# Reordering one step of a fused retention and shrink kernel: another order of the engines' work in the steps with 256-column up products, GpSimd's sums one step behind

## The chip, the cores and the metric

One core of a Trainium2 chip runs the whole program in one launch. The metric is device time in microseconds (us), the median of a few executions. Beside it stands one profiled execution, whose span (first to last instruction) is a little shorter than its own time.

## The reference, cut to what matters

Two parts in a row. The first is a retention block: for 4 batches, 8 heads, 768 positions and head size 64 it keeps a decaying state and reads it with q. Its output, seen as 3072 tokens of 512 values, is the input x of the second part:

```python
h = x @ w_in            # 512 -> 2048
g = h - np.tanh(h)
out = g @ w_out         # 2048 -> 512
```

This case is about the second part, and of that about the stretch in which the first part is already over.

## The kernel before, in words

**Tiling.** The tokens are cut into 12 groups n of 256, the 2048 columns of `h` into 8 pairs m2 of 2 x 128. A tile (n, m2) is 128 partitions x 512 values of `h`: it is made by "up" products on TensorE into PSUM, turned into `g` by ScalarE and VectorE, and consumed by "down" products on TensorE. All is float32. The queues of the engines are in the order in which the program is written out (the schedule is manual): each engine works through its own list, and waits are semaphores between the lists.

**Seven products for eight.** Up and down products use Strassen's scheme (in Winograd's form): 7 block products in place of 8, paid for by sums of blocks. For up products the sums of token blocks are made on GpSimd (`up_tokens`, `block_tokens`, lines 776 to 824), the sums of weights earlier. For down products GpSimd makes four sums of each `g` tile (`fast_sums`, lines 637 to 646, four instructions); products 1, 2 and 4 take `g` itself, products 3, 5, 6 and 7 take a sum.

**Down products as a stream.** `waiting` is the list of tiles whose down products are still to be issued, n by n; the eight tiles of one n are a run and accumulate into one set of PSUM pieces. `next_products(k)` (line 877) issues the next k of the stream. When a tile's last product is issued, `feed()` (line 907) issues GpSimd's sums for those of the next three tiles that are in the set `shrunk`. When a run ends, `fast_end(n)` (line 723) reads the accumulators: `p1` (a copy on ScalarE), then on VectorE `c11`, `v`, and then, as pieces taken from the list `ending`, `w`, `c22`, `x`, `c21`, `c12`, with the stores. Groups 7 to 10 use the same accumulators, so the next run's first products wait for these reads.

**Steps with 128-column products** (n = 4 to 7, lines 1086 to 1158; for n = 6 and 7 the down products come from the stream). A step makes one tile: 8 up products ("U": 1, 5, 7, 6, two matmuls each), `up_take` (ScalarE copies the PSUM bank), `up_pairs` (GpSimd), some down products, 6 more up matmuls ("V": 2, 3, 4) into the same bank, which therefore wait for the copy; `up_add` on VectorE, tanh and square on ScalarE, and the rest of the shrink. At (n, m2) = (7, 2) the four token sums of the first block are issued, in a row.

**Steps with 256-column products** (lines 1180 to 1222; called block steps j = 0 to 15 here). A block is two groups n: block 4 is groups 8 and 9 (j = 0 to 7), block 5 is groups 10 and 11 (j = 8 to 15). Step j makes two tiles at once, A of group 2b and B of group 2b+1, with m2 = j mod 8: U is 8 matmuls of 256 columns, `block_take` copies both banks (ScalarE, two copies), `block_pairs` adds them (GpSimd), V is 6 matmuls into the copied banks, `block_add` adds to them (VectorE: first one for A, then two for B). Then, for each tile: tanh `th` and square `u`, further squares `q0` and `q1` and the mask `large` on ScalarE, and five operations on VectorE, called f0 to f4 here: f0 `th = h - th` (line 502), f1 and f2 multiply by factors (lines 506, 515), f3 multiplies by `u` into `g` (line 543), f4 `copy_predicated` puts `th` where |h| is large (line 544). The last steps of tile B (q1, large, f2 to f4) are done in the next step, after U (`rest(*before)`). Down products are issued in two places of a step: 4 after U, and after V as many as a running count `aim` asks for (10 a step in block 4, 14 in block 5). For the next block, one of four token sums is issued in each of the steps j = 4 to 7.

Of the kernel before, what the change touches and what calls it, by code (L numbers as in the profile page):

```python
# [10 lines left out]
I32 = mybir.dt.int32  # L11
U32 = mybir.dt.uint32
U16 = mybir.dt.uint16
AF = mybir.ActivationFunctionType
# [17 lines left out]
def kernel(  # L32
# [437 lines left out]
    def shrink_begin(n, m2):  # L470
        hp = hps[n, m2]
        u, th = (work(x, 2) for x in ("u", "th"))
        if n < FAST_UP:
            nc.scalar.activation(u, hp, AF.Square)
            nc.scalar.activation(th, hp, AF.Tanh)  # L475
        else:
            nc.scalar.activation(th, hp, AF.Tanh)  # L477
            nc.scalar.activation(u, hp, AF.Square)
        shrinking[n, m2] = [u, th]

    def shrink_factor(n, m2):
        q0 = work("q0", 1)
        nc.scalar.activation(q0, shrinking[n, m2][0], AF.Square, bias=bias0)  # L483
        shrinking[n, m2].append(q0)

    def shrink_factors(n, m2):
        u = shrinking[n, m2][0]
        if n < FAST_UP:
            shrink_factor(n, m2)
        large, q1 = work("large", 2), work("q1", 1)  # L490
        nc.scalar.activation(q1, u, AF.Square, bias=bias1, scale=math.sqrt(A))  # L491
        nc.scalar.activation(large, u, AF.Relu, bias=bias_m)  # L492
        shrinking[n, m2] += [q1, large]

    def shrink_multiply(n, m2):
        shrink_two(n, m2)
# [1 line left out]

    def shrink_two(n, m2):
        hp = hps[n, m2]  # L500
        th = shrinking[n, m2][1]
        nc.vector.tensor_tensor(th, hp, th, op=ALU.subtract)  # L502

    def shrink_third(n, m2):
        hp = hps[n, m2]
        nc.vector.scalar_tensor_tensor(hp, in0=shrinking[n, m2][2], scalar=C0, in1=hp,  # L506
                                       op0=ALU.add, op1=ALU.mult)

    def shrink_last_factor(n, m2):

        hp = hps.pop((n, m2))
        q1 = shrinking[n, m2][3]
        g = gT[n, m2] = new_g(n, m2)
        dst = hp if n < FAST_UP else g.rearrange("p i t -> p (i t)")
        nc.vector.scalar_tensor_tensor(dst, in0=q1, scalar=A * C1, in1=hp, op0=ALU.add,
                                       op1=ALU.mult)
        shrinking[n, m2].append(dst)

    units = []

# [17 lines left out]
        return units.pop(0) if units else next(rooms_for_g)  # L538

    def shrink_end(n, m2):  # L540
        u, th, _, _, large, src = shrinking.pop((n, m2))
        flat = gT[n, m2].rearrange("p i t -> p (i t)")
        nc.vector.tensor_tensor(flat, src, u, op=ALU.mult)
        nc.vector.copy_predicated(flat, large.bitcast(I32), th)  # L544
# [267 lines left out]
    def block_tokens(b):  # L812


        x = xT[b]
        b11, b12, b21, b22 = (x[:, ds(2 * c, 2), ts(i, TH)] for c in range(2) for i in range(2))
        room = op.tile([P, 2, 2, TH], F32, tag="sum", name=f"x_block_{b}")
        t2, t3 = (room[:, i] for i in range(2))
        t4 = odd_room[3].rearrange("p (b c t) -> p b c t", b=2, c=2)[:, b % 2]
        x_of["block", b] = (b11, b21, b22, t4, b12, t2, t3)  # L820
        return [
            lambda d=d, x=x, y=y: nc.gpsimd.tensor_tensor(d, x, y, op=ALU.subtract)
            for d, x, y in ((t3, b22, b12), (b12, b12, b11), (t2, b22, b12), (t4, b21, t2))
        ]
# [219 lines left out]
    for n in range(FAST_UP + 1, PAIRED):  # L1044
        at_ = FIRST_UP - 1 if n == FAST_UP + 1 else PAIRS * (n - 1) + 2
        with_sums.setdefault(at_, []).append(lambda n=n: more_tokens(n))
    def first_block():
        for make in block_tokens(PAIRED // 2):
            make()

    with_sums.setdefault(PAIRS * (PAIRED - 1) + 2, []).append(first_block)
    before = None

    def middle():
# [31 lines left out]
    for s in range(BEGUN, steps.index((PAIRED, 0, True, False))):  # L1086
        n, m2, first, last = steps[s]
        fast = n >= FAST_UP
        ci = with_chunk.get(s)

        falls_back = s == FALL or s in behind_up
        lag = LAG + int(s >= FALL)
        if ci is not None and not falls_back:
            chunk_step(ci)
        if s + 1 in with_chunk:
            for which in range(2):
                scale(with_chunk[s + 1] + 3, which, nc.gpsimd)
        for i in with_weights.get(s, []):
            convert(i)
        if fast:  # L1100
            fast_up(n, m2, (1, 5, 7, 6))
            up_take(n, m2)
        else:
            for i in range(2):
                up(n, m2, i)
        if falls_back and ci is not None:
            chunk_step(ci)
        if before and ci is not None:
            turn_and_see(ci)
        if ci == NCH - 2:  # L1110
            outputs(ci + 1)
            see(ci + 1)
        for i in with_weights.get(s, []):
            load_weights(i + 3)
        waiting.append(steps[s])
        if fast:
            if before and ci is None:
                shrink_factors(*before)
                shrink_last_factor(*before)
            up_pairs()  # L1120
            for make in with_sums.get(s, []):
                make()
            if n < PAIRED - 2:
                downs(lag, 0)
            else:
                next_products(4)
                end_run()
            fast_up(n, m2, (2, 3, 4))
            up_add(n, m2)
            shrink_begin(n, m2)  # L1130
            if before:
                shrink_end(*before)
                if before[0] >= FAST:
                    shrunk.add(before)
                    if n < PAIRED - 2:
                        fast_sums(*before)
                    else:
                        feed()
            if n < PAIRED - 2:
                downs(lag, 1)  # L1140
            else:
                next_products(2)
                end_run()
            end_some(1 + 2 * (n == PAIRED - 1))
            shrink_two(n, m2)
            before = n, m2
            if s + 1 not in with_chunk:
                middle()
        else:
            shrink_begin(n, m2)  # L1150
            shrink_factors(n, m2)
            shrink_multiply(n, m2)
            downs(lag)
            shrink_last_factor(n, m2)
            shrink_end(n, m2)
            for make in with_sums.get(s, []):
                make()
# [2 lines left out]


    def begin(n, m2):
        shrinking[n, m2] = [work(x, 2) for x in ("u", "th")]

    def activated(n, m2, i):
        nc.scalar.activation(shrinking[n, m2][i], hps[n, m2], (AF.Square, AF.Tanh)[i])

    def rest(n, m2):
        shrink_factors(n, m2)
        shrink_last_factor(n, m2)  # L1170
        shrink_end(n, m2)
        shrunk.add((n, m2))
        feed()

    for n in range(PAIRED, 2 * NB):
# [4 lines left out]
    for j in range((NB - FIRST_BLOCK) * PAIRS):  # L1180
        b, m2 = FIRST_BLOCK + j // PAIRS, j % PAIRS
        one, other = (2 * b, m2), (2 * b + 1, m2)
        for i, x in enumerate((one, other)):
            hps[x] = bank("h", "h_%d_%d" % x) if j % 2 else fast_o[i]
        block_up(b, m2, (1, 7, 5, 6))
        block_take(b, m2)
        block_pairs()
        near = left_in_run() <= 7
        next_products(left_in_run() if near else 4)
        rest(*before)  # L1190
        end_run()
        end_some(len(ending))
        if m2 == PAIRS // 2 and b + 1 < NB:
            tokens = block_tokens(b + 1)
        block_up(b, m2, (2, 4, 3))
        aim += 10 if j < PAIRS else 14
        if not near:
            next_products(min(left_in_run(), aim - made[0]))
        if m2 >= PAIRS // 2 and tokens:
            tokens.pop(0)()  # L1200
        block_add(b, m2, [(0, 1)])
        begin(*one)
        activated(*one, 1)
        activated(*one, 0)
        block_add(b, m2, [(1, 0), (1, 1)])
        begin(*other)
        activated(*other, 1)
        shrink_two(*one)
        end_run()
        end_some(len(ending))  # L1210
        shrink_factor(*one)
        shrink_third(*one)
        shrink_factors(*one)
        shrink_last_factor(*one)
        shrink_end(*one)
        shrunk.add(one)
        feed()
        activated(*other, 0)
        shrink_two(*other)
        shrink_factor(*other)  # L1220
        shrink_third(*other)
        before = other
    rest(*before)
    next_products(left_in_run())
    end_run()
    end_some(len(ending))
    LAST = 3
# [63 lines left out]
```

## Time and profile before

| | before |
|---|---|
| median of 3 runs (lowest, highest) | 696.23 us (694.76, 696.40) |
| profiled execution: its own time, its span | 696.99 us, 694.9 us |
| TensorE busy, share of the span | 684.3 us, 98% |
| VectorE busy | 534.2 us, 77% |
| ScalarE busy | 427.3 us, 61% |
| GpSimd busy | 358.3 us, 52% |
| TensorE clock granted | full in every slice |

The steps (6, 0) to (7, 7) lie at about 387 to 480 us of the span, the block steps at 480 to 661 us, and then come the last down products, whose last matmul ends at about 691.7 us. In the profile PE is TensorE, PEld its weight loads, DVE VectorE, ACT ScalarE, POOL GpSimd, SP the queue of the stores and loads. "Idle before <-releaser" is the time for which an engine stood still and what it waited for.

### The profile page before, as it was taken

Reading aid. Unit: us, or ns where it says so; the run is one execution under the profiler, and the core shown is the slowest. Engines: PE = TensorE matmul, PEld = TensorE weight load, DVE = VectorE, ACT = ScalarE, POOL = GpSimd, SP = SyncE. Lnnn points to the kernel's source line nnn. Section 1 sums busy time; section 2 is a strip of 40 time slices with the busy share of each in tenths; the row PEclk is TensorE's granted clock in tenths of the full one; section 3 lists DMA queues with packets and bytes.
Section 4 is the critical chain, followed back from the end, with each engine's and each line's share of the span. In section 5 each row is a group of like instructions: output and inputs, shape, how many; then the busy total and the mean of one; then the engine's idle time right before and its main releaser. Section 6 shows DMA issues by size and latency. Waiting matters only on the chain.

```text
span 694.9 us, 15471 instructions
## 1 busy us (share of the span) xinstructions
PE 684.3 (98%) x6092; PEld 556.4 (80%) x6092; DVE 534.2 (77%) x879; ACT 427.3 (61%) x817; POOL 358.3 (52%) x492
## 2 busy tenths in 40 slices
PE   8999999999999999999999999999999999999998
PEld 5776666667667667789999999989888888888887
DVE  4899989988988965577776687787879888758741
ACT  3687677776766755456555566656766556557510
POOL 1632455444455586887853464554454456444371
PEclk9999999999999999999999999999999999999999
DMA  8992368958878557500000000000000000000000
GB/s 225 232 276 57 92 153 224 228 145 231 236 173 236 149 159 199 138 33 1 1 1 16 17 1 16 16 0 32 1 1 31 1 1 30 1 0 31 1 31 31
DMA packets 119544, 59.89 MB, mean 86 GB/s; under 512 B 101680, under 2 KB 112560, under 8 KB 119472
## 3 DMA queue, kind: packets, MB, share of 16 engines
q1 hardware_dynamic: 116736, 50.08, 27.9%
q10 hardware_dynamic: 2736, 8.83, 3.4%
q8 instruction: 48, 0.79, 0.5%
q14 instruction: 24, 0.20, 0.1%
HBM read 35.83 MB, written 14.68 MB: 73 GB/s over the span
## 4 chain that ended last, share of the span: by engine, by line
PE 88%; DMA 3%; POOL 3%; SPq 2%; ACT 2%; DVE 2%; issue 1%; ACTq 0%; DVEq 0%; POOLq 0%
PE h L464 15%; PE o L552 15%; PE h L793 12%; PE fast_t L692 11%; PE y L692 8%; PE fast_o L832 7%; PE h L832 6%; PE fast_o L692 5%; PE y L398 3%; PE last_h L692 1%; PE s L349 1%; PE s L343 1%; SPq L159 1%; DMA rows<-apart 1%; DMA raw<-in_moe_w_in_dram 1%
## 5 line engine op out<-in xcount | busy, mean ns | idle before, releaser
L464 PE MATMUL h<-xT,w 128*128 128x256 f32 x512 | 117.9, 382 | 0.7 <-ACT xT L444 0.7
L552 PE MATMUL o<-w,g 128*128 128x512 f32 x256 | 116.5, 596 | 0.0
L464 PEld LDWEIGHTS h<-xT,w 128*128 128x128 f32 x512 | 95.9, 190 | 22.4 <-issue 9.1
L552 PEld LDWEIGHTS o<-w,g 128*128 128x128 f32 x256 | 47.5, 190 | 46.2 <-issue 43.0
L483 ACT ACTIVATE q<-u,tab 128x512 f32<-128x512 f32 x88 | 63.7, 724 | 4.5 <-DVE fast_o L506 2.1
L502 DVE TENSOR_TENSOR th<-h,th 128x512 f32<-128x512 f32 x72 | 49.2, 683 | 20.2 <-ACT th L475 17.7
L477 ACT ACTIVATE th<-h 128x512 f32<-128x512 f32 x32 | 19.1, 597 | 73.1 <-DVE h L810 73.1
L208 POOL TENSOR_TENSOR low<-low,power 128x512 f32<-128x512 f32 x26 | 34.1, 1313 | 57.8 <-DVE power L201 42.1
L491 ACT ACTIVATE q<-u,tab 128x512 f32<-128x512 f32 x88 | 63.6, 722 | 0.0
L492 ACT ACTIVATE large<-u,tab 128x512 f32<-128x512 f32 x88 | 62.8, 714 | 0.0
L544 DVE COPY_PREDICATED g<-large,th 128x512 f32<-128x512 int32 x62 | 54.6, 880 | 6.2
L506 DVE SCALAR_TENSOR_TENSOR h<-q,h 128x512 f32<-128x512 f32 x72 | 49.7, 690 | 6.1 <-ACT q L483 6.1
L842 POOL TENSOR_TENSOR fast_head<-fast_head 128x512 f32<-128x512 f32 x16 | 21.4, 1339 | 63.9 <-ACT fast_head L838 63.9
L642 POOL TENSOR_TENSOR s<-g 128x128 f32<-128x128 f32 x38 | 17.8, 469 | 57.5 <-DVE g L544 56.7
L217 POOL TENSOR_TENSOR w<-low,head 128x512 f32<-128x512 f32 x28 | 36.6, 1307 | 14.7 <-DVE low L208 7.6
L793 PEld LDWEIGHTS h<-xT,w 128*128 128x128 f32 x256 | 38.0, 191 | 6.2 <-ACT fast_head L798 1.9
L793 PE MATMUL h<-xT,w 128*128 128x128 f32 x256 | 39.6, 277 | 0.7 <-ACT fast_head L798 0.7
L808 DVE TENSOR_TENSOR h<-h,fast_head 128x256 f32<-128x256 f32 x32 | 13.8, 432 | 33.6 <-PE h L793 25.5
L803 POOL TENSOR_TENSOR fast_head<-fast_head 128x256 f32<-128x256 f32 x32 | 23.4, 730 | 27.5 <-ACT fast_head L798 27.5
L282 POOL TENSOR_TENSOR q<-q,tab 128x512 f32<-128x512 f32 x16 | 17.1, 1066 | 38.7 <-DMA q<-in_q_dram 32.8
L282 POOL TENSOR_TENSOR v<-v,tab 128x512 f32<-128x512 f32 x21 | 24.3, 1157 | 21.3 <-DMA v<-in_v_dram 20.2
L444 ACT COPY xT<-y 128x256 f32<-128x256 f32 x48 | 15.5, 378 | 29.9 <-PE y L398 29.9
(297 smaller groups left out, 1793.2 us busy)
## 6 DMA issues: line engine op xcount, KB each, us to landing
rows<-apart ACTq DMA_DIRECT2D x16, 512.0 KB, 4.5
k<-in_k_dram SPq DMA_DIRECT2D x24, 256.0 KB, 4.4
q<-in_q_dram SPq DMA_DIRECT2D x24, 256.0 KB, 4.7
v<-in_v_dram SPq DMA_DIRECT2D x24, 256.0 KB, 5.7
raw<-in_moe_w_out_dram SPq DMA_DIRECT2D x12, 512.0 KB, 4.3
out_dram<-sum SPq DMA_DIRECT2D x22, 256.0 KB, 2.2
raw<-in_moe_w_in_dram SPq DMA_DIRECT2D x14, 256.0 KB, 4.2
raw<-in_moe_w_in_dram SPq DMA_DIRECT2D x28, 128.0 KB, 4.1
```

What stands on the lines that cost most here:

```text
L282: engine.tensor_tensor(out_, t, g, op=ALU.mult)
L464: nc.tensor.matmul(hp, w1[:, c, ts(2 * m2 + i, P)], xT[n // 2][:, c, ts(n % 2, TH)], start=(begins and c == 0), stop=(c == NC - 1), skip_g ...
L483: nc.scalar.activation(q0, shrinking[n, m2][0], AF.Square, bias=bias0)
L491: nc.scalar.activation(q1, u, AF.Square, bias=bias1, scale=math.sqrt(A))
L492: nc.scalar.activation(large, u, AF.Relu, bias=bias_m)
L502: nc.vector.tensor_tensor(th, hp, th, op=ALU.subtract)
L506: nc.vector.scalar_tensor_tensor(hp, in0=shrinking[n, m2][2], scalar=C0, in1=hp, op0=ALU.add, op1=ALU.mult)
L544: nc.vector.copy_predicated(flat, large.bitcast(I32), th)
L552: nc.tensor.matmul(o_p[n, j], gT[n, m2][:, i, ts(j, P)], w2[:, 2 * m2 + i], start=(first and i == 0), stop=(last and i == 1))
L692: nc.tensor.matmul(accs[n][k], left[k - 1], right, start=first and k in (1, 6, 7, 4), stop=last, skip_group_check=True)
L793: nc.tensor.matmul(hps[n, m2][:, ts(PLACE[k], P)], s_of[m2][k - 1][:, c], x_of[n][k - 1][:, c], start=(k == 1 and c == 0), stop=(c == 1), ...
L832: nc.tensor.matmul(hps[2 * b + i, m2][:, ts(place, TH)], s_of[m2][k - 1][:, c], x_of["block", b][k - 1][:, c], start=(k in (1, 5) and c == 0),
```

## The change

It rewrites the loop over block steps. The order within a step is now a string of pieces, worked through for each step; `-` is tile B of the step before, `A` and `B` the two tiles of this one.

```diff
-        block_up(b, m2, (1, 7, 5, 6))
-        block_take(b, m2)
-        block_pairs()
-        near = left_in_run() <= 7
-        next_products(left_in_run() if near else 4)
-        rest(*before)
-        end_run()
-        end_some(len(ending))
...
-        block_up(b, m2, (2, 4, 3))
-        aim += 10 if j < PAIRS else 14
-        if not near:
-            next_products(min(left_in_run(), aim - made[0]))
...
-        shrink_end(*one)
-        shrunk.add(one)
-        feed()
-        activated(*other, 0)
-        shrink_two(*other)
-        shrink_factor(*other)
-        shrink_third(*other)
+        aim += AIM[j]
+        for piece in order.split():
+            block_pieces[piece](b, m2, one, other, before)
         before = other
```

```python
order = """U M c P q1- s l- f2- V f3- aA thA uA q0A E aB f0A x f4- q1A f1A thB f2A S uB f0B lA f3A f4A q0B f1B"""
AIM = (9, 14, 8, 10, 15, 11, 11, 8, 15, 13, 14, 15, 13, 12, 16, 8)

def more_products():                       # piece E
    if not ended:
        some = min(left_in_run(), aim - made[0])
        next_products(left_in_run() if left_in_run() - some < 6 else some)

def end_sums():                            # piece S
    end_run()
    end_some(len(ending))

def ripe():                                # piece s
    shrunk.update(fresh)
    fresh.clear()
    feed()
```

U and V are the up products, M is `next_products(4)`, c `block_take`, P `block_pairs`, x a token sum of the next block, aA and aB `block_add`; l is `large`. A tile enters `fresh` when its f4 is issued, and `shrunk` only at the next s, so GpSimd's sums for it are issued a step later.

In the steps with 128-column products two things change. The token sums of the first block are spread, one each over (7, 2) to (7, 5). And the down products are grouped otherwise where few are left in a run:

```diff
-                next_products(4)
+                near = left_in_run() if left_in_run() <= 6 else 4
+                next_products(near)
                 end_run()
...
-                next_products(2)
-                end_run()
+                if near == 4:
+                    next_products(6 - 4)
+                    end_run()
```

The last lines after the loop do the remaining pieces of the last tile B, then the rest of run 10, as before. The dictionary in place of a list in `shrinking` changes no instruction.

More of the change, by code (lines that the diff above doesn't have):

```diff
@@ L478, in shrink_begin @@
             nc.scalar.activation(u, hp, AF.Square)
-        shrinking[n, m2] = [u, th]
+        shrinking[n, m2] = {"u": u, "th": th}
     def shrink_factor(n, m2):
         q0 = work("q0", 1)
-        nc.scalar.activation(q0, shrinking[n, m2][0], AF.Square, bias=bias0)
-        shrinking[n, m2].append(q0)
+        nc.scalar.activation(q0, shrinking[n, m2]["u"], AF.Square, bias=bias0)
+        shrinking[n, m2]["q0"] = q0
     def shrink_factors(n, m2):
-        u = shrinking[n, m2][0]
+        u = shrinking[n, m2]["u"]
         if n < FAST_UP:
@@ L492, in shrink_factors @@
         nc.scalar.activation(large, u, AF.Relu, bias=bias_m)
-        shrinking[n, m2] += [q1, large]
+        shrinking[n, m2].update(q1=q1, large=large)
     def shrink_multiply(n, m2):
@@ L500, in shrink_two @@
         hp = hps[n, m2]
-        th = shrinking[n, m2][1]
+        th = shrinking[n, m2]["th"]
         nc.vector.tensor_tensor(th, hp, th, op=ALU.subtract)
@@ L505, in shrink_third @@
         hp = hps[n, m2]
-        nc.vector.scalar_tensor_tensor(hp, in0=shrinking[n, m2][2], scalar=C0, in1=hp,
+        nc.vector.scalar_tensor_tensor(hp, in0=shrinking[n, m2]["q0"], scalar=C0, in1=hp,
                                        op0=ALU.add, op1=ALU.mult)
@@ L511, in shrink_last_factor @@
         hp = hps.pop((n, m2))
-        q1 = shrinking[n, m2][3]
+        q1 = shrinking[n, m2]["q1"]
         g = gT[n, m2] = new_g(n, m2)
@@ L516, in shrink_last_factor @@
                                        op1=ALU.mult)
-        shrinking[n, m2].append(dst)
+        shrinking[n, m2]["src"] = dst
     units = []
@@ L540, in shrink_end @@
     def shrink_end(n, m2):
-        u, th, _, _, large, src = shrinking.pop((n, m2))
+        u, th, large, src = (shrinking[n, m2][x] for x in ("u", "th", "large", "src"))
+        del shrinking[n, m2]
         flat = gT[n, m2].rearrange("p i t -> p (i t)")
@@ L1046, with first_block @@
         with_sums.setdefault(at_, []).append(lambda n=n: more_tokens(n))
[L1047 to L1051, printed above, removed]
+    begun_tokens = []
+    def first_block(i):
+        if not i:
+            begun_tokens.extend(block_tokens(PAIRED // 2))
+        begun_tokens.pop(0)()
+    for i in range(4):
+        with_sums.setdefault(PAIRS * (PAIRED - 1) + 2 + i, []).append(lambda i=i: first_block(i))
     before = None
@@ L1162, in begin, with activated @@
     def begin(n, m2):
[L1163 to L1172, printed above, removed]
+        shrinking[n, m2] = {x: work(x, 2) for x in ("u", "th")}
+    def activated(n, m2, x, how):
+        nc.scalar.activation(shrinking[n, m2][x], hps[n, m2], how)
@@ new lines, in tanh, with shrink_q1, shrink_large, shrink_gated @@
+    def tanh(n, m2):
+        begin(n, m2)
+        activated(n, m2, "th", AF.Tanh)
+    def shrink_q1(n, m2):
+        q1 = work("q1", 1)
+        nc.scalar.activation(q1, shrinking[n, m2]["u"], AF.Square, bias=bias1, scale=math.sqrt(A))
+        shrinking[n, m2]["q1"] = q1
+    def shrink_large(n, m2):
+        large = work("large", 2)
+        nc.scalar.activation(large, shrinking[n, m2]["u"], AF.Relu, bias=bias_m)
+        shrinking[n, m2]["large"] = large
+    def shrink_gated(n, m2):
+        u, src = (shrinking[n, m2][x] for x in ("u", "src"))
+        nc.vector.tensor_tensor(gT[n, m2].rearrange("p i t -> p (i t)"), src, u, op=ALU.mult)
@@ new lines, in shrink_small @@
+    def shrink_small(n, m2):
+        u, th, large, src = (shrinking[n, m2][x] for x in ("u", "th", "large", "src"))
+        del shrinking[n, m2]
+        nc.vector.copy_predicated(gT[n, m2].rearrange("p i t -> p (i t)"),
+                                  large.bitcast(I32), th)
+        fresh.append((n, m2))
+    def more_products():
[3 more added lines that the diff above has]
+    def end_sums():
+        end_run()
+        end_some(len(ending))
@@ new lines, in some_tokens @@
+    def some_tokens(b, m2):
+        if m2 == PAIRS // 2 and b + 1 < NB:
+            tokens.extend(block_tokens(b + 1))
+        if tokens:
+            tokens.pop(0)()
+    of_tile = {
+        "th": tanh, "u": lambda *x: activated(*x, "u", AF.Square), "q0": shrink_factor, "q1": shrink_q1,
+        "l": shrink_large, "f0": shrink_two, "f1": shrink_third, "f2": shrink_last_factor,
+        "f3": shrink_gated, "f4": shrink_small,
+    }
+    block_pieces = {
+        "U": lambda b, m2, *_: block_up(b, m2, (1, 7, 5, 6)),
+        "V": lambda b, m2, *_: block_up(b, m2, (2, 4, 3)),
+        "c": lambda b, m2, *_: block_take(b, m2),
+        "P": lambda *_: block_pairs(),
+        "s": lambda *_: ripe(),
+        "x": lambda b, m2, *_: some_tokens(b, m2),
+        "M": lambda *_: next_products(4),
+        "E": lambda *_: more_products(),
+        "S": lambda *_: end_sums(),
+        "aA": lambda b, m2, *_: block_add(b, m2, [(0, 1)]),
+        "aB": lambda b, m2, *_: block_add(b, m2, [(1, 0), (1, 1)]),
+        **{x + "A": lambda b, m2, one, *_, f=f: f(*one) for x, f in of_tile.items()},
+        **{x + "B": lambda b, m2, one, other, *_, f=f: f(*other) for x, f in of_tile.items()},
+        **{x + "-": lambda *at_, f=f: f(*at_[-1]) for x, f in of_tile.items()},
+    }
@@ L1173, in rest @@
+    order = """U M c P q1- s l- f2- V f3- aA thA uA q0A E aB f0A x f4- q1A f1A thB f2A S uB f0B lA f3A f4A q0B f1B"""
+    AIM = (9, 14, 8, 10, 15, 11, 11, 8, 15, 13, 14, 15, 13, 12, 16, 8)
+    fresh = []
+    def ripe():
+        shrunk.update(fresh)
+        fresh.clear()
         feed()
@@ L1184 @@
             hps[x] = bank("h", "h_%d_%d" % x) if j % 2 else fast_o[i]
-        block_up(b, m2, (1, 7, 5, 6))
-        block_take(b, m2)
-        block_pairs()
-        near = left_in_run() <= 7
-        next_products(left_in_run() if near else 4)
-        rest(*before)
-        end_run()
-        end_some(len(ending))
-        if m2 == PAIRS // 2 and b + 1 < NB:
-            tokens = block_tokens(b + 1)
-        block_up(b, m2, (2, 4, 3))
-        aim += 10 if j < PAIRS else 14
-        if not near:
-            next_products(min(left_in_run(), aim - made[0]))
[L1199 to L1214, printed above, removed]
-        shrink_end(*one)
-        shrunk.add(one)
-        feed()
-        activated(*other, 0)
-        shrink_two(*other)
-        shrink_factor(*other)
-        shrink_third(*other)
+        aim += AIM[j]
+        for piece in order.split():
+            block_pieces[piece](b, m2, one, other, before)
         before = other
-    rest(*before)
+    ripe()
+    for piece in ("q1", "l", "f2", "f3", "f4"):
+        of_tile[piece](*before)
     next_products(left_in_run())
+    ripe()
     end_run()
```

## The prediction

> **What bounds the kernel now.** I read the page's first part, then the waits of TensorE (PE), then PE's timeline in the stretch that the diff touches.
>
> ```profile
> PE 684.3 (98%) x6092; PEld 556.4 (80%) x6092; DVE 534.2 (77%) x879; ACT 427.3 (61%) x817; POOL 358.3 (52%) x492
> ```
>
> PE is busy nearly always, and the change removes no matmul. So the most that it can gain is the time in which PE stands still between 387 us (step (6, 0)) and the end. Busy shares of the others average over stages and settle nothing here.
>
> How full is "busy"? In PE's timeline a 256-column matmul starts 0.432 us after the one before (block step 11 starts at 600.72 and step 12 at 612.81: 12.09 us for 28 matmuls), a 128-column one 0.2225 us. I took every start-to-start distance and subtracted these; what exceeds them is stall. There are two such places in the 128-column steps and two in the block steps, each seen as an idle note:
>
> ```profile
> 459.59 0.71 PE L793 MATMUL h<-xT,w 128*128 128x128 f32 x4 [0.50 <-ACT fast_head L798]
> 464.24 1.13 PE L692 MATMUL fast_t<-w,g_x 128*128 128x256 f32 x4 [0.39 <-DVE sum L709]
> 568.75 1.13 PE L832 MATMUL fast_o<-xT,w 128*128 128x256 f32 x4 [0.49 <-ACT fast_head L838]
> 579.82 1.10 PE L692 MATMUL fast_t<-w,g_x 128*128 128x256 f32 x4 [0.45 <-DVE sum L709]
> ```
>
> By starts they cost 0.77, 0.66, 0.76 and 0.69 us (each with a slow first matmul after the wait, some 0.1). A hiccup at 468.3 adds 0.07, four in the block steps (525.6, 557.7, 581.6, 630.1) 0.4. Sums: **1.5 us in the 128-column steps, 1.8 in the block steps, 3.3 in all**. That is the ceiling. Behind the last matmul lie 3.2 us of adding and storing that the change leaves alone.
>
> Why does PE stand there? Before 459.59, GpSimd (POOL) makes the four token sums at once:
>
> ```profile
> 447.36 1.27 POOL L822 TENSOR_TENSOR x_block<-xT 128x512 f32<-128x512 f32 x1
> 448.71 1.27 POOL L822 TENSOR_TENSOR xT<-xT 128x512 f32<-128x512 f32 x1
> 450.06 1.80 POOL L822 TENSOR_TENSOR x_block<-xT 128x512 f32<-128x512 f32 x1
> 451.94 1.62 POOL L822 TENSOR_TENSOR x_first<-xT,x_block 128x512 f32<-128x512 f32 x1
> ...
> 456.06 0.43 DVE L808 TENSOR_TENSOR h<-h,fast_head 128x256 f32<-128x256 f32 x1 [1.62 <-POOL fast_head L803]
> 457.22 0.60 ACT L477 ACTIVATE th<-h 128x512 f32<-128x512 f32 x1 [3.45 <-DVE h L810]
> ```
>
> The pair sum (L803) of the next step queues behind them, VectorE's add behind it, tanh behind that, and ScalarE's copy of the next bank behind tanh; V waits for the copy. The stall at 464.24 is the end of run 6 (c11 late) on top. At 568.75 it is the same chain one block later:
>
> ```profile
> 559.76 1.72 DVE L543 TENSOR_TENSOR g_x<-g_x,u 128x512 f32<-128x512 f32 x1
> 561.59 1.63 DVE L544 COPY_PREDICATED g_x<-large,th 128x512 f32<-128x512 int32 x1
> ...
> 569.02 0.46 POOL L642 TENSOR_TENSOR s<-g 128x128 f32<-128x128 f32 x1 [6.40 <-DVE g L544]
> 573.37 1.26 POOL L842 TENSOR_TENSOR fast_head<-fast_head 128x512 f32<-128x512 f32 x1
> ```
>
> f3 and f4 (0.69 and 0.75 us elsewhere) stretch beside pair and token sums; GpSimd waits 6.40 us at its queue's head for a `g`, makes two tiles' sums, and so the next pair sum, ready to go from about 569.2, runs at 573.37.
>
> **What the Trainium skill says.** "SBUF — State Buffer", section Who interferes with whom: VectorE with two SBUF inputs and GpSimd reading SBUF exclude each other. The trace agrees in kind: f3 0.69 alone, 1.72 here. "Perfetto Trace Analysis", section Optimizing Scalar/DVE Operations: unsaturated VectorE and ScalarE can still cause bubbles on other engines. So it is here, at 77% and 61%.
>
> **The change part by part.** Counts of matmuls, activations, VectorE and GpSimd operations and DMAs stay (192 down products over the 16 steps as before; after them 20 of run 10 are left, not 14, since the block now begins 6 products behind). Only places move.
>
> *Token sums one per step, (7, 2) to (7, 5).* GpSimd then has 0.73 pair sum + 1.3 to 1.8 token + at most 1.8 of down sums = 4.3 in a step of 5.7 us. The first stall goes: **-0.77**.
>
> *Run ends in the first half of a step.* `near` moves two products from (6, 3) to (6, 4), and run 6 now ends in (7, 5), a step with 2 products. Such steps are short: (7, 5) is U 1.78 + 0.86 + V 1.34 = 3.98 us, (6, 3) 4.4. But ScalarE does not get shorter: p1, c11 and v stand ahead of the add and so of tanh, square, q0 and the copy. Step (6, 3) of the trace has this order already; its U starts at 404.39, and the next step's copy is
>
> ```profile
> 412.22 0.57 ACT L798 COPY fast_head<-h 128x512 f32<-128x512 f32 x1
> ```
>
> so it ends 8.40 us after U starts. V of the next step wants it at 3.98 + 1.78 + 1.73 = 7.49 after (7, 5), and, since V of (6, 3) ends at 408.81 and U of (6, 4) would now follow at once, at 408.81 + 1.78 + 1.73 = 412.32; the copy ends at 412.79. The stalls: 0.9 + 0.1 restart = **+1.0** at (7, 6), 0.5 + 0.1 = **+0.6** at (6, 4). In exchange c11 of run 6 comes at 4.4, before run 7's first product at 5.8: **-0.66**, with the hiccup **-0.07**. The 128-column steps together: -0.77 - 0.73 + 1.6 = **+0.1**. Behind (7, 6), w, c22, x, c21 and c12 (0.35 each) delay VectorE, but by my addition (7, 7)'s copy is 0.5 early.
>
> *The block steps.* I put the new order on a step's clock (U at 0, M 3.45, V 5.17 to 7.76) with durations from steps 10 and 11. Copies end at 4.2 and the pair sum at 5.6, as now (605.04 for a step that starts at 600.72). VectorE: f2- 4.95, f3- 5.65, aA 7.0, aB to 8.7, f0A, f4- to 10.05, f1A, f2A to 11.3, f0B, f3A, f4A to 13.45, f1B to 14.1, which is 2.0 in a step of 12.09 us and 4.6 in the shortest (9.5). The next f2- is at 4.95: it fits. With a run's end in it (steps 3, 8, 12) seven adds of 0.35 come ahead of f0B: f1B ends 5.0 into the next step, f3- at 6.4, aA still at 7.0. ScalarE: thB is held by f4- (same buffer) to 10.1, q0B ends at 12.55, and the copy that V needs has over 0.8 us of slack in all steps. GpSimd: the pair sum goes first, and the sums behind it are of tiles whose f4 ended in the step before, so nothing waits at its head. Are the sums in time, a step later? (8, 4) is summed in step 5 by 7.5 and first used in step 6; (8, 7) is done by 7.5 in step 8, and its product 6 comes at 10.35; (10, 7)'s s2 is ready at 14.8 and needed at 16.4. The token sum of step 7 now starts at 7.5, behind f3-, and can meet aB and f4-: about 1 us, within what I counted free. After the run ends in steps 3, 8 and 12 VectorE has read the first two pieces by 12.1, the next run wants them at 3.45 of the next step. So all 1.8 us of stall can go; I leave 0.2 for hiccups at waits: **-1.6**.
>
> Stores and SP: out stores move by a step with the run ends and end long before the last ones; **0**, the tail hides them. The tail's sums of run 11 on GpSimd (1.8 a tile against 3.0 of PE) stay ahead.
>
> **Sum:** +0.1 - 1.6 = -1.5 us. The profiled execution has 2.1 us around its span: 694.9 - 1.5 + 2.1 = 695.5. It was 0.8 above the median; for the median 696.2 - 1.5 = **694.7**.
>
> **The unknowns, bounded.** The two short-step stalls: 0 (if tanh comes earlier because less is queued) to 2.4 (each half as long again). The block steps: -1.8 (every stall gone) to 0, or more if VectorE falls behind.
>
> **The rivals.** *Short steps cost nothing:* 8.40 came from a step whose f3 and f4 ran 1.21 and 1.10 beside GpSimd's sums, so the true chain may be shorter; against it, p1 waited on ScalarE's queue, not on those. Then -1.5 - 1.6 = -3.1: 693.1. *The stalls only change place,* the short steps at their 2.4 and block steps saving half: about 0, 696.2. For it speaks that each stall seen is a delay of the same chain. *Slower:* VectorE, in steps 4 to 7. Its work is 8.3 us a step, token sums can stretch aB, f0A, f3, f4 by 1 to 2 us, and step 7 lasts only 9.5 us. From lateness of 0.6 at aA, tanh and the next copy move too; past 0.6 + 2.2 (ScalarE's slack), V of every further step waits. At 1 us in each of four steps, the rest as now, it gives 696.2 + 4 = 700.2. Against it, the same work fits now with one visible stall.
>
> **How the numbers follow.** Forecast 0.48 (693.8 to 695.6 its own range), short steps free 0.24, change of place 0.14, slower 0.14. A measurement of this kernel can tell 0.3%, 2.1 us. Faster than 694.1 are nearly all of the second case and a quarter of the first: 0.36; slower 0.14; the rest 0.50. The range 692.9 to 697.6 leaves out the slower case and a little below.
>
> **What would show it.** After: no idle note near 459 and 568 to 580; new ones of 0.6 and 1.0 us on V of (6, 4) and (7, 6) behind ScalarE's copy; GpSimd's waits for f4 (76 us now over the kernel, 30 in this stretch) gone from the block steps. Wrong if the short steps do not stall, or if V of steps 5 to 9 waits for copies.

## The result, and the profile after

| | before | after |
|---|---|---|
| median of 22 runs each (lowest, highest) | 696.45 us (694.28, 697.69) | 694.43 us (692.92, 696.29) |
| ratio after / before | | 0.9977, 95% interval 0.9968 to 0.9986 |
| profiled execution: own time, span | 696.99, 694.9 us | 695.49, 693.7 us |

The change takes 1.6 us off (0.0023 of 696.45; 1.0 to 2.2 by the ends of the interval). The means of the 22 runs differ by 1.6 too, the medians by 2.0. The forecast was 1.5. As a share it is 0.23%, less than the 0.3% for which the chances were given, although with so many runs the interval leaves out 1.

Busy times say nothing of it, as before:

```profile
PE 684.3 (99%) x6092; PEld 556.7 (80%) x6092; DVE 531.7 (77%) x879; ACT 429.2 (62%) x817; POOL 356.1 (51%) x492
```

So I read TensorE's starts again. This is its timeline after, in the 128-column steps (start, duration, engine, line, operation; in brackets the idle time shown and its releaser). The lines are the first matmuls of U of (6, 4), V of (6, 4), V of (7, 5), V of (7, 6) and U of (7, 7):

```profile
409.17 0.68 PE L794 MATMUL h<-xT,w 128*128 128x128 f32 x4
...
412.98 0.71 PE L794 MATMUL h<-xT,w 128*128 128x128 f32 x4
...
463.94 0.71 PE L794 MATMUL h<-xT,w 128*128 128x128 f32 x4
...
469.50 0.71 PE L794 MATMUL h<-xT,w 128*128 128x128 f32 x4 [0.38 <-ACT fast_head L799]
...
472.04 0.68 PE L794 MATMUL h<-xT,w 128*128 128x128 f32 x4
```

By start-to-start distances, including the slow first group after each wait, they cost 0.29, 0.32, 0.39, 0.65 and 0.30 us; a hiccup at U of (7, 6) adds 0.06. That is 2.0 us where before had 1.5, and only one of the five has an idle note. What released them, judged by the times of their ends, is in the timelines of ScalarE and VectorE:

```profile
412.36 0.57 ACT L799 COPY fast_head<-h 128x512 f32<-128x512 f32 x1
...
463.32 0.57 ACT L799 COPY fast_head<-h 128x512 f32<-128x512 f32 x1
...
468.88 0.57 ACT L799 COPY fast_head<-h 128x512 f32<-128x512 f32 x1
```

```profile
408.33 0.69 DVE L515 SCALAR_TENSOR_TENSOR g<-q,h 128x512 f32<-128x512 f32 x1
...
471.20 0.69 DVE L515 SCALAR_TENSOR_TENSOR g<-q,h 128x512 f32<-128x512 f32 x1
```

The three copies end at 412.93, 463.89 and 469.45, each 0.05 ahead of a V. The two f2 end at 409.02 and 471.89, each 0.15 ahead of a U: they are the last readers of the PSUM bank of the tile two steps earlier, which that U writes.

In the block steps nothing is left. Here is TensorE where V of step 8 and, behind U of step 9, the next run's first product waited before; now both follow without a gap (0.432 us a matmul) or a note:

```profile
568.09 0.59 PE L693 MATMUL y<-fast_kqT,s 128*128 128x256 f32 x2
568.52 1.03 PE L833 MATMUL fast_o<-xT,w 128*128 128x256 f32 x4
...
578.02 1.03 PE L833 MATMUL h<-x_block,fast_raw 128*128 128x256 f32 x4
578.88 1.07 PE L693 MATMUL fast_t<-w,g_x 128*128 128x256 f32 x4
```

GpSimd there now has the pair sum ahead of the tile's sums, and waits for the copy it needs in place of a `g`:

```profile
567.68 1.28 POOL L843 TENSOR_TENSOR fast_head<-fast_head 128x512 f32<-128x512 f32 x1 [4.91 <-ACT fast_head L839]
568.92 0.45 POOL L643 TENSOR_TENSOR s<-g 128x128 f32<-128x128 f32 x1
```

Its waits over the block steps after (what waited, for what: us in total, times, longest):

```profile
POOL fast_head L843 <- ACT fast_head L839: 83.0, 16, 9.6
POOL s L643 <- PE fast_t L693: 10.2, 7, 1.6
POOL s L643 <- DVE g L1196: 0.7, 1, 0.7
```

Before, the same table had two waits for `g` and two for `g_x` (22.8 us together, each up to 6.4); 0.7 is left. And of the long VectorE operations, the same f3 and f4 in step 7 take now

```profile
559.46 0.94 DVE L1191 TENSOR_TENSOR g_x<-g_x,u 128x512 f32<-128x512 f32 x1
...
563.58 0.72 DVE L1196 COPY_PREDICATED g_x<-large,th 128x512 f32<-128x512 int32 x1
```

in place of 1.72 and 1.63: f3 no longer runs beside the pair sum and f4 no longer beside a token sum.

### The profile page after: what moved, and what is told of

Read it like the earlier page. It is cut to its first block, busy times and chain, and to the rows that moved or that the text cites. A ratio compares the mean times of both kernels' runs of the same rounds, so it can differ in the third digit from the quotient of the medians.

```text
span 693.7 us, 15451 instructions
## 1 busy us (share of the span) xinstructions
PE 684.3 (99%) x6092; PEld 556.7 (80%) x6092; DVE 531.7 (77%) x879; ACT 429.2 (62%) x817; POOL 356.1 (51%) x492
## 4 chain that ended last, share of the span: by engine, by line
PE 89%; DMA 3%; ACT 2%; SPq 2%; DVE 2%; issue 1%; POOL 1%; ACTq 0%; DVEq 0%; POOLq 0%
PE o L553 15%; PE h L464 15%; PE h L794 12%; PE fast_t L693 12%; PE y L693 8%; PE h L833 7%; PE fast_o L833 7%; PE fast_o L693 5%; PE y L398 3%; PE last_h L693 1%; PE s L349 1%; PE s L343 1%; SPq L159 1%; DMA rows<-apart 1%; DMA raw<-in_moe_w_in_dram 1%
## 5 line engine op out<-in xcount | busy, mean ns | idle before, releaser
L483 ACT ACTIVATE q<-u,tab 128x512 f32<-128x512 f32 x88 | 63.6, 723 | 1.4
L545 DVE COPY_PREDICATED g<-large,th 128x512 f32<-128x512 int32 x51 | 47.0, 922 | 5.0
L643 POOL TENSOR_TENSOR s<-g 128x128 f32<-128x128 f32 x40 | 19.2, 480 | 44.3 <-DVE g L545 39.6
L491 ACT ACTIVATE q<-u,tab 128x512 f32<-128x512 f32 x55 | 39.7, 722 | 0.0
L492 ACT ACTIVATE large<-u,tab 128x512 f32<-128x512 f32 x55 | 39.2, 713 | 0.0
```

Source lines behind the costliest of these rows:

```text
L483: nc.scalar.activation(q0, shrinking[n, m2]["u"], AF.Square, bias=bias0)
```

## The experiments

**How they are measured.** Profiled executions of one kernel differ by more than the effects here, and most of that lies ahead of the changed steps: from the start of the span to the U that stands at 381.09 in before (one step ahead of (6, 0)) the kernels of this study took 378.7 to 382.4 us, with nothing changed there. So beside the timed ratio I give the **stretch** from that U to the start of TensorE's last recorded matmuls, and TensorE's **stall** in it, by starts, in the 128-column and in the block steps. Each ratio is against runs of before on the same chip; its us are its distance from 1 times 696.

| kernel | stretch, against before's 309.13 | stall 128-col. + block | ratio (95%) | us |
|---|---|---|---|---|
| before | 0 | 1.50 + 1.83 | 1 | 0 |
| after | -1.33 | 2.01 + 0.0 | 0.9977 (0.9968, 0.9986) | -1.6 |
| tokens_spread | -0.81 | 0.70 + 1.73 | 0.9990 (0.9980, 1.0000) | -0.7 |
| run_ends | +4.75 | 1.9 + 6.3 | 1.0081 (1.0062, 1.0101) | +5.6 |
| block_only | -1.77 | 1.51 + 0.0 | 0.9974 (0.9961, 0.9986) | -1.8 |
| spread_and_block | -2.58 | 0.70 + 0.0 | 0.9959 (0.9944, 0.9975) | -2.9 |
| sums_at_once | -0.23 | 2.0 + 1.13 | 0.9987 (0.9976, 0.9997) | -0.9 |
| sums_behind | -1.47 | 1.5 + 0.30 | 0.9972 (0.9962, 0.9983) | -1.9 |
| run_ends_caught_up | +0.32 | 1.94 + 1.81 | 1.0001 (0.9989, 1.0012) | +0.1 |
| lag_and_spread | -2.28 | 0.71 + 0.32 | 0.9976 (0.9961, 0.9991) | -1.7 |
| early_p1 | -3.26 | 0.07 + 0.0 | 0.9950 (0.9928, 0.9971) | -3.5 |

Stretch and stall move together within about 0.1 us in every row. That alone proves little, because both are read from the same starts of the same trace: it says that the plain spacing of the matmuls is the same in all kernels. What stands on its own is the timed ratio, and in every row its interval holds the difference of the stretch.

### tokens_spread: the token sums alone

Before, with the four token sums spread over (7, 2) to (7, 5):

```diff
-    with_sums.setdefault(PAIRS * (PAIRED - 1) + 2, []).append(first_block)
...
+    for i in range(4):
+        with_sums.setdefault(PAIRS * (PAIRED - 1) + 2 + i, []).append(lambda i=i: first_block(i))
```

> The kernel before with one edit: the first block's four token sums spread over steps (7, 2) to (7, 5). Theory (each stall is a late pair sum or a late accumulator read): the stall of 0.77 us near 459 goes, and the one of 0.66 near 464 with it, because the late c11 came from the same token sums; PE's stalls in the 128-column steps fall from 1.5 to about 0.1 us, the block steps keep their 1.8; time -1.4 us. Rival (c11 is late because run 6 ends in the second half of a step): only 0.77 goes, time -0.8 us.

The stretch lost 0.81 us: the stall at 459.59 went, and no more, as the rival had it. The wait for c11 of run 6 stays, as TensorE's timeline of this kernel shows:

```profile
461.90 1.13 PE L692 MATMUL fast_t<-w,g_x 128*128 128x256 f32 x4 [0.36 <-DVE sum L709]
```

So that wait does not come from the token sums. That it comes from where run 6 ends is shown by run_ends, where it is gone, and by early_p1 below.

### run_ends: the grouping of down products alone

Before, with `near` in n = 6 and 7:

```diff
-                next_products(4)
+                near = left_in_run() if left_in_run() <= 6 else 4
+                next_products(near)
...
-                next_products(2)
-                end_run()
+                if near == 4:
+                    next_products(6 - 4)
+                    end_run()
```

> The kernel before with one edit: the new grouping of down products where few are left in a run (n = 6 and 7). Theory: the short steps cost what they cost in the changed kernel, 0.6 us at (6, 4) and 1.4 around (7, 6), the stall near 459 stays at 0.77 and the one at 464 goes: the 128-column steps rise from 1.5 to 2.8 us, the block steps keep about 1.8; time +1.3 us. Rival (the grouping was there to free run 7's first product, and its short steps are covered): time 0 to -0.7 us.

It is 5.6 us slower, far from every expectation, and 4.5 us of new stall (6.3 for 1.83) lie in the block steps, which the edit does not touch. TensorE's waits there (same columns as GpSimd's above):

```profile
PE fast_o L832 <- ACT fast_head L838: 3.1, 2, 1.6
PE h L832 <- ACT fast_head L838: 2.4, 1, 2.4
```

The first of the three, in TensorE's timeline, and what stands ahead of its copy on VectorE and ScalarE:

```profile
532.72 1.13 PE L832 MATMUL h<-xT,w 128*128 128x256 f32 x4 [2.42 <-ACT fast_head L838]
```

```profile
524.54 0.40 DVE L709 TENSOR_TENSOR sum<-fast_t,fast 128x256 f32<-128x256 f32 x1
...
526.76 0.42 DVE L709 TENSOR_TENSOR sum<-fast_t,fast 128x256 f32<-128x256 f32 x1
527.10 0.76 DVE L848 TENSOR_TENSOR fast_o<-fast_o,fast_head 128x256 f32<-128x256 f32 x2
```

```profile
527.55 0.60 ACT L1168 ACTIVATE th<-fast_o 128x512 f32<-128x512 f32 x1 [4.62 <-DVE fast_o L848]
...
532.10 1.05 ACT L838 COPY fast_head<-h 128x512 f32<-128x512 f32 x2
```

With `near`, the block steps begin 6 products behind. Run 7 then has 7 or fewer left when step 4 begins, so by before's own rule it ends in the step's first half: all its accumulator reads (seven VectorE operations, 524.54 to 527.10, 2.6 us) stand ahead of the adds that tanh waits for, and tanh ahead of the next step's copy. Runs 8 and 9 do the same in steps 9 and 13 (stalls of 1.83 us each at V of the steps behind them).

### run_ends_caught_up: the same, the backlog taken off in the first block step

run_ends, with 16 in place of 10 products aimed at in step 0:

```diff
-        aim += 10 if j < PAIRS else 14
+        aim += (16 if j == 0 else 10) if j < PAIRS else 14
```

> The new grouping in n = 6 and 7 on the kernel before, as in the run with that edit alone (8.2 us of stall, of which 6.3 in block steps), and in the first block step 16 down products in place of 10, so that from step 1 on the stream stands where it stood before and the runs end again in the second half of a step. Theory (the 6.3 us come from run ends in the first half of block steps, not from the short steps): stalls of 1.9 us in the 128-column steps and 1.8 in the block steps, time +0.4 us against before. Rival (the late start of the block costs by itself): 3 us or more stay in the block steps, time +2 us or more.

The block stall falls from 6.3 back to 1.8, before's own. So the backlog was the cause, and the list `AIM`, whose first two numbers make up 6 products, is what keeps it from showing in the changed kernel. Alone, `near` gains nothing (+0.1 us, interval -0.8 to +0.8).

### block_only and spread_and_block: the new block steps without `near`

After, with before's grouping in n = 6 and 7; spread_and_block keeps the spread token sums, block_only has them in a row too:

```diff
-    AIM = (9, 14, 8, 10, 15, 11, 11, 8, 15, 13, 14, 15, 13, 12, 16, 8)
+    AIM = (8, 9, 8, 10, 15, 11, 11, 8, 15, 13, 14, 15, 13, 12, 16, 8)
```

> The changed kernel's block steps behind the 128-column steps of before (tokens in a row, old grouping). The first two counts of down products are 8 and 9 in place of 9 and 14, since 6 products more are already made. Theory: block steps without a stall, 128-column steps with their 1.5 us: time -1.8 us against before. Rival (the block gain needs the other start): stalls of 0.5 us or more in steps 0 to 3, time -1 us or less.

> As the changed kernel, but with the old grouping of down products in n = 6 and 7 (first two counts 8 and 9). Theory: no short steps, so about 0.1 us of stall in the 128-column steps and none in the block steps: time -3.2 us against before, 1.2 to 1.9 below the changed kernel. Rival (the late c11 comes back at 464): 0.7 us of stall, time -2.5 us.

block_only: the whole block stall, 1.83 us, goes, the 128-column steps stay (1.51). spread_and_block adds the 0.81 of the token sums and has one wait left, c11 of run 6, as its rival expected, in its TensorE timeline:

```profile
462.71 1.13 PE L693 MATMUL fast_t<-w,g_x 128*128 128x256 f32 x4 [0.36 <-DVE sum L710]
```

Its stretch is 1.25 us shorter than after's (306.55 against 307.80). `near` costs 2.0 us of short-step stalls there and takes away 0.7. The timed ratios (0.9959 and 0.9977) point the same way, though their intervals overlap.

### sums_at_once: the new order, GpSimd's sums not put off

After, with the sums issued as soon as f4 is:

```diff
-        fresh.append((n, m2))
+        shrunk.add((n, m2))
+        feed()
```

> The changed kernel with one edit: GpSimd's sums for a tile are issued at once when its f4 is issued, not a step later. Theory (the order within the step has slack of its own): GpSimd again waits at its queue's head for f4, the pair sum comes up to 2 us later in a step, but aA and the copies have 0.6 + 2.2 us of slack, so block steps stall by 0 to 0.4 us; time within 0.4 us of the changed kernel. Rival (the lag of one step carries the gain): the stalls near step 8 return, 1.4 us, time near the changed kernel + 1.4.

Block stall 1.13. GpSimd's timeline at step 8 shows the old picture, a wait for `g` at the queue's head and the pair sum behind it; VectorE's add and TensorE follow:

```profile
565.52 0.46 POOL L643 TENSOR_TENSOR s<-g 128x128 f32<-128x128 f32 x1 [6.05 <-DVE g L1196]
...
569.53 1.27 POOL L843 TENSOR_TENSOR fast_head<-fast_head 128x512 f32<-128x512 f32 x1
```

```profile
570.84 0.76 DVE L849 TENSOR_TENSOR fast_o<-fast_o,fast_head 128x256 f32<-128x256 f32 x2 [2.93 <-POOL fast_head L843]
```

```profile
577.92 1.10 PE L693 MATMUL fast_t<-w,g_x 128*128 128x256 f32 x4 [0.89 <-DVE sum L710]
```

The copies were ready at 565.57, so the pair sum ran 4 us late, which I had put at 2 at most. The stall came at the next run's first product, not at V. The new order, with the counts of `AIM`, takes 0.7 of the 1.83 without the lag.

### sums_behind: the old order, GpSimd's sums put off

Before, with the tile entering `fresh` and the sums issued behind the next step's pair sum:

```diff
         block_pairs()
+        ripe()
...
-        shrunk.add(one)
-        feed()
+        fresh.append(one)
```

(`rest`, for tile B, is edited in the same way.)

> The kernel before with one edit: in the block steps GpSimd's sums are issued a step behind, after the pair sum; VectorE's and ScalarE's order and the counts of down products stay. If the lag carries the gain: the two stalls near 568 and 579 go, block steps stall by 0 to 0.3 us in place of 1.8, time -1.6 us. If the new order carries it: 1.4 us or more of stall stays, time 0 to -0.4 us.

GpSimd's timeline: pair sum first, no wait for `g`.

```profile
565.01 1.28 POOL L842 TENSOR_TENSOR fast_head<-fast_head 128x512 f32<-128x512 f32 x1 [5.03 <-ACT fast_head L838]
566.25 0.45 POOL L642 TENSOR_TENSOR s<-g 128x128 f32<-128x128 f32 x1
```

Block stall 0.30, three hiccups of 0.10. So the lag alone brings 1.5 of the 1.83, the rest of the rewrite 0.3 on top.

How the lag does it differs between the two large stalls. The one at 579.82 is the wait at the queue's head: the pair sum at 573.37 was late, the add behind it (574.67) too, and the reads of run 8 behind that. Ahead of the one at 568.75 the pair sum was done in time, at 560.94. But, made behind a tile's sums, it ran together with f3, and the token sum with f4 (the two lines of 1.72 and 1.63 us in the prediction), and VectorE's adds stood in its own queue behind these, until 563.11. With the lag only a tile's small sums meet f3 and f4:

```profile
556.44 0.69 DVE L543 TENSOR_TENSOR g_x<-g_x,u 128x512 f32<-128x512 f32 x1
557.24 0.82 DVE L544 COPY_PREDICATED g_x<-large,th 128x512 f32<-128x512 int32 x1
```

The adds begin at 557.95, 7.8 us after the step's U in place of 10.6. Of these 2.8 us, 1.8 are the shorter f3 and f4, and 1.0 is that f2 itself began earlier.

### lag_and_spread: two small edits in the old kernel

sums_behind with the token sums of tokens_spread (both diffs above).

> The kernel before with two edits: the sums a step behind in the block steps, and the first block's token sums spread. Theory (stalls add): 0.7 us at the end of run 6 and 0.3 of hiccups stay, 1.0 in place of 3.3; time -2.3 us against before, with the old order within the step. Rival (the new order is needed as well): 1.8 us or more stay.

-2.28 us of stretch: 1.5 and 0.8 add up. By the stretch these two small edits are worth 0.95 us more than the whole change. The timed -1.7 has an interval of -2.7 to -0.6, too wide to confirm that.

### early_p1: the last wait, by another edit

spread_and_block, with p1 and c11 of run 6 issued a half-step early, in (7, 4) ahead of the last products, which they do not depend on:

```diff
+                if (n, m2) == (PAIRED - 1, 4):
+                    fast_begin(PAIRED - 2)          # p1 and c11 only
...
-            todo[x]()
+            if x == "v" or n != PAIRED - 2:
+                todo[x]()
```

> As the run with old grouping, spread tokens and new block steps (0.7 us of stall, at the end of run 6), with one more edit: p1 and c11 of run 6 are issued in the first half of step (7, 4), where ScalarE and VectorE stand idle, not at its end. Theory: run 7's first product finds its accumulator free, PE's stalls from 380 us on fall to 0.1 us or less; time -3.3 us against before. Rival (the wait is passed to v, or c11 delays the add and with it a copy): 0.4 us or more stay.

In the timelines of ScalarE, VectorE and TensorE p1 ends at 460.88, c11 at 461.33, and the next run's first product follows U at 464.18 with no idle note:

```profile
460.91 0.42 DVE L710 TENSOR_TENSOR sum<-fast_t,fast 128x256 f32<-128x256 f32 x1 [0.18 <-ACT fast L716]
```

```profile
464.18 1.03 PE L693 MATMUL fast_t<-w,g_x 128*128 128x256 f32 x4
```

0.07 us of stall remain of 3.3. Median 692.67 us against 696.68 for before on the same chip: the lowest median and the shortest stretch of all, below before beyond doubt. Against after the stretch says 1.93 us less (305.87 and 307.80); the two timed intervals just touch (up to 0.9971, from 0.9968).

## Why the prediction was right or wrong, point by point

**The ceiling, 3.3 us: right.** early_p1 empties it but for 0.07, and its stretch is 3.26 us shorter.

**Token sums, -0.77: right.** Alone they brought -0.81; that GpSimd's four sums in a row cause this stall is thereby shown.

**c11 of run 6 and the hiccup, -0.66 and -0.07: right in kind.** Both are gone after, and the wait survives in every kernel without `near` but early_p1. They are gone because run 6 ends where its first reads come early.

**Short steps, +0.6 and +1.0: the step that was mis-sized.** At (6, 4) 0.61 was lost, as predicted, but half of it at U. At the end of run 6 V of (7, 6) lost 0.65 and V of (7, 5) 0.39, in place of 1.0 at V of (7, 6) alone: I had only asked what follows the short step, and left out that the short step's own V comes sooner after its U. U of (7, 6) and of (7, 7) lost 0.06 and 0.30 more. The kind of wait that I missed is U's: a short step brings the next U forward too, and it needs the bank that f2 of the tile two steps earlier reads last. Altogether 2.0 in place of 1.6, so the 128-column steps came to +0.5 (2.01 - 1.50), not +0.1. That (7, 7)'s copy would be about 0.5 early was right: V of (7, 7) did not wait.

**Block steps, -1.6: right, 0.2 too careful.** All 1.83 went; the 0.2 kept for hiccups was not needed. The reason holds: the lag of GpSimd's sums is what does it (sums_behind, 1.5 of 1.83). The new order leans on that lag more than I expected: with the sums at once it stalls for 1.13. The prediction's lines for 568.75 mix two chains: the long f3 and f4 belong to that stall, the wait of 6.40 us to the one at 579.82 (see sums_behind). Of the signs, GpSimd's waits for f4 in the block steps fell from 22.8 us to 0.7; the "30 in this stretch" counts only waits for `g`, and with those for `g_x` it is 42.3 from 387 to 661 us.

One reading of the clock was wrong, and that it cost nothing is luck. The prediction has the first two pieces of a run read by 12.1 us, and the next run's first product wanting them only at 3.45 of the next step, which is 15.5. But the reads wait for the run's last product and p1: after, in step 8, p1 stood waiting for TensorE until 575.63 and c11 for p1 until 576.03, which is 12.7 us into the step. And it is the last read that counts, not the second. In before that read is

```profile
579.26 0.42 DVE L709 TENSOR_TENSOR sum<-fast_t,fast 128x256 f32<-128x256 f32 x1
```

It ends at 579.68, c11 ended at 577.43, and TensorE goes on at 579.82. The piece read last and the one written first are both in the tile `fast_t`; that this is the reason is not tested. After, the same read is

```profile
578.28 0.42 DVE L710 TENSOR_TENSOR sum<-fast_t,fast 128x256 f32<-128x256 f32 x1
```

It ends at 578.70, 15.36 us into step 8, and the next run's first product starts at 578.88. TensorE had started 0.14 us after the end of that read where it waited (before, and sums_at_once), so some 0.04 us were to spare in place of more than 3. The other two run ends in the block steps have the same 0.18. VectorE's next add (aA of step 9) came 8.3 us into its step, not 7.0, which ScalarE's slack covered.

**The sum.** Two errors of opposite sign, +0.4 and -0.2, nearly cancel: the stretch says -1.33, the timing -1.6, the forecast -1.5. That they lie so close is in part luck.

**The rivals.** Short steps are not free (2.0 us). "The stalls only change place" is true of the 128-column steps and false of the block steps. VectorE late in steps 4 to 7 did not occur. The side on which I looked for a slower result did hold a real mechanism, though another one: run ends in the first half of block steps, +4.5 us in run_ends, from which `AIM` protects the changed kernel. The prediction counted that the block begins 6 products behind and saw no more in it than a longer tail.

## What to carry to other kernels

On the engine that bounds a kernel, subtract the plain spacing of its instructions from their start-to-start distances: the sum is the ceiling of what reordering can bring on that engine. Read in each kernel's trace from a common instruction on, it resolves 0.1 us here, where single runs of one kernel scatter by 3; the timed ratio remains the check. An operation that waits at the head of an in-order queue holds up everything behind it (6.4 us here), so issue it a step later, behind what the next step needs at once. A sum on GpSimd also decides by its place how long VectorE's operations beside it take, and these can stand ahead of what TensorE waits for. When a step gets shorter, check all that it brings forward: its own second half, the next step's first buffer, and where the backlog that it leaves makes later bursts of work fall.

## What the runs showed of the hardware that I had not expected

- A matmul group after a wait is slow beyond the wait itself: 0.71 us where the same four 128-column records take 0.61, 1.13 where four 256-column records take 1.03. And the idle note understates a stall: 0.38 shown at 469.50 where starts give 0.54, none at 463.94 where they give 0.28.
- The program up to the U ahead of step (6, 0), the same instructions in every kernel, took 378.7 to 382.4 us from one profiled execution to another. That is more than twice the effect of the change, so spans of single profiles could not have settled it.
- VectorE's operations with all inputs in SBUF stretch by where GpSimd's sums fall, and those with an input in PSUM did not here. From 387 us on in before, f3 took 0.68 to 0.69 us in the 30 cases with no sum beside it, and up to 1.75 beside the 128x512 sums; f4 took 0.73 to 0.76, and up to 1.64. f0 and f2, which have one input in PSUM, took at most 0.70 in the 60 cases with a sum beside them. In total VectorE's busy time fell by only 2.5 us of 534.2, but f3 and f4 of step 7 stood on the path to the stall at 568.75.
